# Pooled attention and two gated layers on one core: the second layer's block products changed from eight to seven

## The chip, the cores and the metric

One core of one Trainium2 chip. A core has a matrix engine (PE, with its weight loader PEld), a vector engine (DVE), an activation engine (ACT), a general engine (POOL), a queue that only issues transfers (SP), and 16 DMA engines. The metric is device time in microseconds (us) of one execution; lower is better. The kernel before takes 1918.09 us (median of three runs, 1917.99 to 1919.66).

## The reference

```python
def _attn_ref(q, k, v):                 # 8 batches, 8 heads, 576 positions, head size 64
    k_p, v_p = mean over groups of 8 positions of k, v
    attn = softmax(q @ k_p.T / sqrt(64))
    return attn @ v_p
def _moe_ref(x, w_in, w_out):           # 4608 tokens, 512 -> 2048 -> 512
    h = x @ w_in
    return (h * clip(h + 3, 0, 6) / 6) @ w_out
def _moe2_ref(x, w_gate, w_val, w_out): # 512 -> 1536 -> 512
    g = x @ w_gate
    return (g / (1 + exp(-g)) * (x @ w_val)) @ w_out
```

The output is `_moe2_ref(_moe_ref(_attn_ref(q, k, v)))`, 4608 x 512 in float32. The weights come as float64.

## The kernel before

Activations are kept transposed: features on the 128 partitions, tokens along the free dimension, in nine blocks of N = 512 tokens. A float32 operand of a large product is held as a pair hi + lo of float32r values, and a product is three matmuls: hi hi, hi lo, lo hi (`mm3`, its matmul is line 460). `split` makes a pair: ACT casts hi (line 118), and DVE or POOL subtracts it for lo (line 119). A weight arrives as 64-bit words in pieces of 128 x 256 and is brought to float32 by bits: ACT rescales it (line 97) and DVE does three integer operations for each piece (`join`, lines 102, 108 and 113). `Weights.convert(n)` moves n pieces through each of the three stages fetched, rescaled, joined.

The order of every engine's instructions is the program's order; nothing is reordered by a planner. A tile pool has a fixed number of buffers, and whoever writes a buffer anew waits for the last reader of its tile before.

First layer: blocks j = 0 to 8, in each the 16 feature tiles f, called slots here. A slot issues `up` (12 matmuls into a bank `h`), half of the attention steps due for the next block (`attn_slot`), `act1` (ACT Relu, line 482, then DVE, line 484), a `convert`, `down1` of the slot two before (12 matmuls into four banks `y`), the other half of the attention steps, `emit_fly` (the split of this slot's down weights, cast on ACT, lo on POOL), `split_g` (g's own split), and a `convert`. Block 0 converts the first layer's weights, block 8 and the second layer's first block convert the second layer's. Attention has two banks of its own (`ps_a`, tag `att`); line 352 is the score product, lines 438 to 441 are attention's last products, lines 449 and 453 split their result into x.

Second layer: for each block j and each f of 12, 12 matmuls `gate`, 12 `val`, the activation (lines 522 to 525), the split of g on ACT and DVE, and 12 matmuls of `down2` of the f before. All its up weights lie in SBUF as pairs, its down weights as float32, split anew for every use by `emit_fly`. That makes 9 x 12 x 36 = 3888 matmuls of 512 columns.

Of the kernel before, what the change touches and what calls it, by code (L numbers as in the profile page):

```python
# [8 lines left out]
F32 = mybir.dt.float32  # L9
# [14 lines left out]
def kernel(  # L24
# [37 lines left out]
    wu_p = ctx.enter_context(tc.tile_pool(name="wu", bufs=F1))  # L62
    wd_p = ctx.enter_context(tc.tile_pool(name="wd", bufs=F1))
    fly_p = ctx.enter_context(tc.tile_pool(name="fly", bufs=2))
    stg_p = ctx.enter_context(tc.tile_pool(name="stg", bufs=6))
    x_p = ctx.enter_context(tc.tile_pool(name="x", bufs=2))
    g_p = ctx.enter_context(tc.tile_pool(name="g", bufs=2))
    t_p = ctx.enter_context(tc.tile_pool(name="t", bufs=2))
    dram = ctx.enter_context(tc.tile_pool(name="dram", bufs=1, space=DRAM))
    ps_y = ctx.enter_context(tc.tile_pool(name="ps_y", bufs=1, space=PSUM))  # L70
    ps_h = ctx.enter_context(tc.tile_pool(name="ps_h", bufs=2, space=PSUM))
    ps_a = ctx.enter_context(tc.tile_pool(name="ps_a", bufs=2, space=PSUM))
# [4 lines left out]
    y_d = [dram.tile([P, KT, N], F32, name=f"y{j}") for j in range(NB)]  # L77

# [1 line left out]
    wu = {}  # L80
    wd = {}
# [11 lines left out]
    # Scaled by 2^-112, the high word's view as float32 has its exponent field  # L93
    # at float32's bias, three bits too low.
# [26 lines left out]
    class Weights:  # L121
        """Pieces of weight tiles, fetched ahead and converted in order."""
# [21 lines left out]
        def convert(self, n=1):  # L144
            """Moves each of three stages on by n pieces, the last stage first."""
            done, self.joined = self.joined, []
            for (kind, key, _, pool, i), t in done:
                if kind == "up":
                    if i == 0:
                        self.cur[key] = pool().tile([P, 2, KT, P], F32R, tag="wu", name="wu")  # L150
                    w = self.cur[key].rearrange("p a k f -> p a (k f)")[:, :, WC * i:WC * (i + 1)]
                    split(w[:, 0], w[:, 1], f32(t), nc.gpsimd)
                if i == KT * P // WC - 1:
                    (wu if kind == "up" else wd)[key] = self.cur.pop(key)
            pieces = []
            scaled, self.scaled = self.scaled, []
            for item, s in scaled:
                kind, key, _, pool, i = item
                if kind == "up":
                    t = t_p.tile([P, WC], I32, tag="w32", name="w32")  # L160
                else:
                    if i == 0:
                        self.cur[key] = wd_p.tile([P, DM], F32, tag="wd", name="wd")
                    t = self.cur[key][:, WC * i:WC * (i + 1)].bitcast(I32)
                pieces.append((s, t))
                self.joined.append((item, t))
# [10 lines left out]
    def emit_fly(key):  # L177
        t = fly_p.tile([P, 2, DM], F32R, tag="fly", name="fly")
        split(t[:, 0], t[:, 1], wd[key], nc.gpsimd)
        fly[key] = t  # L180

# [9 lines left out]
    a_p = attn_ctx.enter_context(tc.tile_pool(name="a", bufs=1))  # L191
# [35 lines left out]
    # The first batch is staged whole, in the up weights' place.  # L227
# [54 lines left out]
    # Before the first block the products' banks are free for the attention.  # L282
# [196 lines left out]
    # first layer  # L479
# [15 lines left out]
    def store_y(j):  # L495
        for d in range(KT):
# [5 lines left out]
            (nc.sync if d % 2 else nc.scalar).dma_start(out=y_d[j][:, d], in_=o)  # L502

    # second layer
    x2_t = {}

    y_t = {}

    def load_y(j):
        for kt in range(KT):  # L510
            y_t[j, kt] = p2["y"].tile([P, N], F32, tag="ystg", name="ystg")
            nc.sync.dma_start(out=y_t[j, kt], in_=y_d[j][:, kt])

    def split_y(j, kt):
        if kt == 0:
            x2_t[j] = x_p.tile([P, KT, 2, N], F32R, tag="x", name="x2")
        x = x2_t[j]
        split(x[:, kt, 0], x[:, kt, 1], y_t.pop((j, kt)), nc.vector)

    def act2(pg, pv):  # L520
        s = t_p.tile([P, N], F32, tag="t", name="s")
        nc.scalar.activation(out=s, in_=pg, func=ACTF.Sigmoid)  # L522
        u = t_p.tile([P, N], F32, tag="g32", name="u")
        nc.vector.tensor_tensor(out=u, in0=s, in1=pg, op=ALU.mult)  # L524
        nc.vector.tensor_tensor(out=u, in0=u, in1=pv, op=ALU.mult)  # L525
        return u

    def down2(j, f):
        if f == 0:
            accumulators((2, j))  # L530
        g, w = g_t.pop((2, j, f)), fly.pop(("out2", f))
        for i in range(N // P):
            mm3(acc[2, j][i], lambda _, a: g[:, a, i * P:(i + 1) * P], lambda _, a: w[:, a],
                [0], f == 0, f == F2 - 1)

    def store_o(j):
        for i in range(N // P):
            o = t_p.tile([P, DM], F32, tag="t" if i % 2 else "g32", name="oo")
            if i % 2:
                nc.vector.tensor_copy(out=o, in_=acc[2, j][i])  # L540
            else:
                nc.scalar.copy(out=o, in_=acc[2, j][i])
            nc.sync.dma_start(out=out[j * N + i * P:j * N + (i + 1) * P, :], in_=o)

# [1 line left out]
    # Attention units (batch, head pair, first query, queries, queries per  # L546
    # tile), none across a block's edge, in the order of the blocks.
# [62 lines left out]
    # The order must keep every stage behind what it reads, and every buffer  # L610
    # until its last reader.
# [112 lines left out]
    def wu_pool():  # L724
        return wu_p

    with tc.manual_schedule():
# [20 lines left out]
        for f in range(F1):  # L748
            weights.add_up(("in", f), w_in, wu_pool, f)
            weights.add_down(("out", f), w_out, f)  # L750
# [5 lines left out]
        while ("out", 0) not in wd:  # L756
            weights.convert(2)
# [9 lines left out]
        early = 8  # L767
        p2 = {}
        seq1 = [(j, f) for j in range(NB) for f in range(F1)]
        for n, (j, f) in enumerate(seq1):  # L770
            if j == NB - 1 and f == 0:
                attn_ctx.close()
                p2["pool"] = ctx.enter_context(tc.tile_pool(name="wu2", bufs=early))
                p2["y"] = ctx.enter_context(tc.tile_pool(name="ystg", bufs=4))
                for m in range(F2):
                    for i, (nm, src) in enumerate((("gate", w_gate), ("val", w_val))):
                        pool = p2["pool"] if 2 * m + i < early else wu_p
                        weights.add_up((nm, m), src, lambda pool=pool: pool, m)
                    weights.add_down(("out2", m), w_out2, m)
# [4 lines left out]
            weights.convert({0: 2, NB - 1: 2}.get(j, 0))  # L784
# [9 lines left out]
            if j == NB - 1 and f == 4:  # L794
                load_y(0)
            if j == NB - 1 and 8 <= f < 8 + KT:
                split_y(0, f - 8)
# [4 lines left out]
        weights.convert(2)  # L802
# [55 lines left out]
```

## Time and profile before

| | |
|---|---|
| median of three runs | 1918.09 us |
| span of the profiled execution, first to last instruction | 1917.7 us |
| PE, PEld busy | 1844.3 (96%), 1520.1 (79%) |
| DVE, ACT, POOL busy | 1052.7 (55%), 707.9 (37%), 630.4 (33%) |
| data moved | 95.96 MB, mean 50 GB/s |
| chain that ended last | PE 81%, DVE 12%, issue 3%, DMA 2%, ACT 1%, POOL 1% |

The page holds the busy shares, the span in 40 slices, and the chain of waits that ended last. Other views group instructions by line and shape, list who waited for whom, show instructions in order of time, or give each engine's busy time in chosen stretches with the clock that PE was granted (1.00 is 2.4 GHz, 0.50 is 1.2 GHz). A busy time counts an instruction from start to end, and waiting for a port lies inside it.

### The profile page before, as it was taken

The page shows a single profiled execution, that of the slowest core. Times are in us where ns is not written, and L with a number is a line of the kernel's source. Part 1 is how long each engine was busy: PE and PEld are TensorE (multiplying, and loading weights), DVE is VectorE, ACT ScalarE, POOL GpSimd, SP SyncE. Part 2 cuts the span into 40 slices and gives each one's busy share as a digit, 9 for nine tenths or more (in the row PEclk, how much of TensorE's full clock was granted, in tenths as well). Part 3 has the DMA queues.
Part 4 walks back from the last instruction along what each step waited for, and adds up shares of the span by engine and source line. Part 5 has one row for each costly group of instructions (what it writes and reads, how often), then busy time and mean ns, then how long its engine had stood idle before and what let it go on. Part 6 is the DMA issues. An engine that isn't in the chain of part 4 may idle for free.

```text
span 1917.7 us, 24136 instructions
## 1 busy us (share of the span) xinstructions
PE 1844.3 (96%) x8525; PEld 1520.1 (79%) x8525; DVE 1052.7 (55%) x1975; ACT 707.9 (37%) x1712; POOL 630.4 (33%) x730
## 2 busy tenths in 40 slices
PE   5787999999999999999988999999999999999999
PEld 4666788888888888788776788888888888888887
DVE  7999676666577766754698723232323332323322
ACT  5444444444444444444454422222222222222222
POOL 5556453535435353622343311111111111111111
PEclk8789999999999999999999999999999999999999
DMA  7443112111111121210245110101010101000000
GB/s 163 122 148 109 47 44 56 44 48 47 43 34 47 49 53 33 45 55 1 88 143 165 55 44 0 45 1 44 1 45 0 44 1 31 14 22 23 8 16 22
DMA packets 136553, 95.96 MB, mean 50 GB/s; under 512 B 84720, under 2 KB 105200, under 8 KB 136432
## 3 DMA queue, kind: packets, MB, share of 16 engines
q1 hardware_dynamic: 131728, 89.43, 16.4%
q10 hardware_dynamic: 4704, 4.98, 0.8%
q8 instruction: 67, 1.10, 0.2%
q14 instruction: 54, 0.44, 0.1%
HBM read 75.50 MB, written 18.87 MB: 49 GB/s over the span
## 4 chain that ended last, share of the span: by engine, by line
PE 81%; DVE 12%; issue 3%; DMA 2%; ACT 1%; POOL 1%; SPq 0%; POOLq 0%; DVEq 0%; ACTq 0%
PE y L460 31%; PE h L460 17%; PE val L460 14%; PE gate L460 14%; DVE w L108 2%; PE pss L352 2%; DVE wd L108 2%; DVE wd L102 2%; DVE w L102 1%; DVE w L113 1%; DVE wd L113 1%; PE pst L412 1%; PE pst L416 1%; DVE g L484 1%; POOL wu L119 1%
## 5 line engine op out<-in xcount | busy, mean ns | idle before, releaser
L119 POOL TENSOR_TENSOR fly<-wd,fly 128x512 fp32r<-128x512 f32 x252 | 331.8, 1317 | 809.1 <-ACT fly L118 804.9
L460 PE MATMUL h<-x,wu 128*128 128x512 f32 x1728 | 439.2, 404 | 9.5 <-DVE g L484 9.5
L460 PE MATMUL y<-g,fly 128*128 128x512 f32 x1728 | 429.1, 397 | 4.5 <-ACT g L118 2.4
L460 PEld LDWEIGHTS h<-x,wu 128*128 128x128 f32 x1728 | 324.7, 193 | 77.3 <-DVE g L484 12.0
L460 PEld LDWEIGHTS y<-g,fly 128*128 128x128 f32 x1728 | 317.5, 189 | 69.1 <-DVE g L119 3.2
L460 PE MATMUL y<-fly,g 128*128 128x512 f32 x1296 | 312.9, 390 | 3.4 <-POOL fly L119 3.4
L460 PE MATMUL gate<-x,wu 128*128 128x512 f32 x1296 | 311.3, 389 | 0.0
L460 PE MATMUL val<-x,wu 128*128 128x512 f32 x1296 | 311.3, 389 | 0.0
L460 PEld LDWEIGHTS y<-fly,g 128*128 128x128 f32 x1296 | 242.8, 188 | 56.1 <-POOL fly L119 5.7
L460 PEld LDWEIGHTS gate<-x,wu 128*128 128x128 f32 x1296 | 243.3, 188 | 50.5
L460 PEld LDWEIGHTS val<-x,wu 128*128 128x128 f32 x1296 | 243.3, 188 | 50.4
L524 DVE TENSOR_TENSOR u<-s,gate 128x512 f32<-128x512 f32 x108 | 74.1, 686 | 340.0 <-ACT s L522 340.0
L522 ACT ACTIVATE s<-gate 128x512 f32<-128x512 f32 x108 | 64.4, 596 | 331.0 <-PE gate L460 331.0
L118 ACT CAST g<-u 128x512 fp32r<-128x512 f32 x108 | 67.0, 621 | 309.2 <-DVE u L525 309.2
L119 DVE TENSOR_TENSOR g<-g,g 128x512 fp32r<-128x512 f32 x128 | 132.7, 1037 | 84.9 <-ACT g L118 84.9
L395 POOL TENSOR_TENSOR e<-e,sm 96x288 f32<-96x288 f32 (+3 forms) x85 | 68.1, 801 | 336.9 <-ACT g L118 151.6
L118 ACT CAST fly<-wd 128x512 fp32r<-128x512 f32 x252 | 155.1, 615 | 27.0 <-PE y L460 26.1
L525 DVE TENSOR_TENSOR u<-u,val 128x512 f32<-128x512 f32 x108 | 74.2, 687 | 135.9 <-PE val L460 135.0
L119 DVE TENSOR_TENSOR g<-u,g 128x512 fp32r<-128x512 f32 x108 | 74.8, 693 | 79.2 <-ACT g L118 79.2
L484 DVE SCALAR_TENSOR_TENSOR g<-t,h 128x512 f32<-128x512 f32 x144 | 97.2, 675 | 30.5 <-ACT t L482 28.7
L382 ACT ACTIVATE e<-e 96x288 f32<-96x288 f32 (+3 forms) x85 | 35.3, 415 | 190.7 <-DVE e L379 188.4
L482 ACT ACTIVATE t<-h,three 128x512 f32<-128x512 f32 x144 | 98.1, 681 | 19.4 <-PE h L460 19.0
(97 smaller groups left out, 1708.8 us busy)
## 6 DMA issues: line engine op xcount, KB each, us to landing
wstg<-in_moe_w_out_dram SPq DMA_DIRECT2D x56, 256.0 KB
ystg<-y SPq DMA_DIRECT2D x36, 256.0 KB
out_dram<-oo SPq DMA_DIRECT2D x36, 256.0 KB
wstg<-in_moe_w_in_dram SPq DMA_DIRECT2D x32, 256.0 KB
k_in<-in_k_dram SPq DMA_DIRECT2D x56, 144.0 KB
wstg<-in_moe_w_gate_dram SPq DMA_DIRECT2D x24, 256.0 KB
wstg<-in_moe_w_val_dram SPq DMA_DIRECT2D x24, 256.0 KB
y<-yo ACTq DMA_DIRECT2D x18, 256.0 KB
```

The source lines that it names most:

```text
L102: nc.vector.tensor_scalar(out=dst, in0=hi, scalar1=4, scalar2=1, op0=ALU.logical_shift_left, op1=ALU.logical_shift_right,)
L108: nc.vector.scalar_tensor_tensor(out=dst, in0=lo, scalar=29, in1=dst, op0=ALU.logical_shift_right, op1=ALU.bitwise_or)
L113: nc.vector.scalar_tensor_tensor(out=dst, in0=hi, scalar=-(2 ** 31), in1=dst, op0=ALU.bitwise_and, op1=ALU.bitwise_or)
L118: nc.scalar.copy(out=hi, in_=src)
L119: lo_engine.tensor_tensor(out=lo, in0=src, in1=f32(hi), op=ALU.subtract)
L395: nc.gpsimd.tensor_tensor(out=e3, in0=e3, in1=sm.to_broadcast(list(e3.shape)), op=ALU.mult)
L460: nc.tensor.matmul(out=ps, lhsT=w(kt, wh), rhs=x(kt, xh), start=first and n == 0, stop=last and n == 3 * len(kts) - 1,)
L482: nc.scalar.activation(out=t, in_=ps, func=ACTF.Relu, bias=three)
L484: nc.vector.scalar_tensor_tensor(out=g, in0=t, scalar=6.0, in1=ps, op0=ALU.min, op1=ALU.mult)
L522: nc.scalar.activation(out=s, in_=pg, func=ACTF.Sigmoid)
L524: nc.vector.tensor_tensor(out=u, in0=s, in1=pg, op=ALU.mult)
L525: nc.vector.tensor_tensor(out=u, in0=u, in1=pv, op=ALU.mult)
```

## The change

The second layer works on six groups of 768 tokens, and each of its three products on 2 x 2 blocks, with seven block products in place of eight (Strassen's scheme in Winograd's form). The sums of weight blocks are built, split into pairs and written to DRAM during the first layer's blocks 1 to 7, one of 18 units in six slots (`prep_step`); in the second layer all of them are streamed back for every group through a ring of four SBUF tiles (`load_up`, `load_dn`). The first layer's down weights are split once, in block 0, written to DRAM, and loaded again for each later slot (`load_fly`).

```diff
-    wd_p = ctx.enter_context(tc.tile_pool(name="wd", bufs=F1))
-    fly_p = ctx.enter_context(tc.tile_pool(name="fly", bufs=2))
+    fly_p = l1.enter_context(tc.tile_pool(name="fly", bufs=3))
...
+    M = 384
+    NG = NT // (2 * M)
+    NPAIR = F2 // 2
...
         def convert(self, n=1):
...
+                if i == 0:
+                    if kind == "up":
+                        self.cur[key] = wu_p.tile([P, 2, KT, P], F32R, tag="wu", name="wu")
+                    else:
+                        self.cur[key] = fly_p.tile([P, 2, DM], F32R, tag="fly", name="fly")
...
+                split(w[:, 0], w[:, 1], f32(t), nc.gpsimd)
                 if i == KT * P // WC - 1:
+                    t = self.cur.pop(key)
+                    (wu if kind == "up" else fly)[key] = t
+                    if kind == "down":
+                        nc.sync.dma_start(out=w1_d[key[1]], in_=f32(t))
...
-    def emit_fly(key):
+    def load_fly(f):
         t = fly_p.tile([P, 2, DM], F32R, tag="fly", name="fly")
-        split(t[:, 0], t[:, 1], wd[key], nc.gpsimd)
+        nc.sync.dma_start(out=f32(t), in_=w1_d[f])
...
+    def prep_step(u, step):
...
+        elif step == 2:
+            q = prep_t["f"] = q7_p.tile([P, 8, WC], F32, tag="q7", name="q7")
+            join([(s, q[:, i].bitcast(I32)) for s, i in prep_t.pop("q")])
...
+        elif step == 4:
+            nc.scalar.copy(out=t[:, :, 0], in_=q[:, :7])
+        else:
+            for a, b, eng in ((0, 4, nc.gpsimd), (4, 7, nc.vector)):
+                eng.tensor_tensor(out=t[:, a:b, 1], in0=q[:, a:b], in1=f32(t[:, a:b, 0]), op=ALU.subtract)
...
+    def x_step(p, n, lo_eng, sum_eng):
...
+        split(x[:, 0], x[:, 1], v(what), lo_eng)
+        if then:
+            sums_b(sum_eng, v, (then,))
...
+    def up2(p, u):
+        f, m = u
+        for what, wa, xb in UP:
+            b = bank()[:, :M]
+            w, x = wr.pop(("up", u, A7[wa])), xc[p, xb]
+            for k in range(2):
+                mm3x(b, lambda a: w[:, a, k], lambda a: x[:, a, k], k == 0, k == 1)
...
+    def split_gc(p, n, c, lo_eng):
+        what = DN[n][1]
+        t = gc[p, n, c] = l2["gc"].tile([P, 2, CH, M], F32R, tag="gc", name="gc")
+        split(t[:, 0], t[:, 1], gf[p][:, GP[what], CH * c:CH * (c + 1)], lo_eng)
+    def sums_g(p, what, eng):
+        h = NPAIR // 2
+        for a in range(0, NPAIR, h):
+            sums_a(eng, lambda q: gf[p][:, GP[q], a:a + h], (what,))
+    def down2(p, n):
+        what = DN[n][0]
+        b = dn_b[what] = [bank()[:, :2 * P] for i in range(PT)]
+        for c in range(NPAIR // CH):
+            g = gc.pop((p, n, c))
+            for t in range(PT):
+                for k in range(CH):
+                    w = wr["dn", n, CH * c + k]
+                    mm3x(b[t], lambda a: g[:, a, k, t * P:(t + 1) * P], lambda a: w[:, a],
+                         c == 0 and k == 0, c == NPAIR // CH - 1 and k == CH - 1)
...
             hp = ps_h.tile([P, N], F32, tag="h", name="h")
             up(hp, wu["in", f], x_tile(j))
             attn_slot(j, 2 * f)
             g = act1(hp)
-            weights.convert({0: 2, NB - 1: 2}.get(j, 0))
+            weights.convert(2 if j == 0 else 0)
             if n >= 2:
                 jd, fd = seq1[n - 2]
                 down1(jd, fd)
...
-            emit_fly(("out", f))
             split_g((1, j, f), g)
-            weights.convert({0: 2, NB - 1: 2 * (f % 2)}.get(j, 0))
+            weights.convert(2 if j == 0 else 0)
+            if j > 0 and n - F1 < PREP_STEPS * len(preps):
+                prep_step((n - F1) // PREP_STEPS, (n - F1) % PREP_STEPS)
+            if j == NB - 1 and f >= 4 and f < 11:
+                x_step(0, f - 4, nc.gpsimd, nc.gpsimd)
...
+        for p in range(NG):
+            for n, (f, m) in enumerate(units2):
+                c = up2(p, (f, m))
+                load_next()
+                if m == 0:
+                    g = gate2(c)
+                else:
+                    val2(p, f, g, c)
+                    if f % CH == CH - 1:
+                        split_gc(p, 0, f // CH, nc.gpsimd)
+                        split_gc(p, 1, f // CH, nc.vector)
+                if n == 2 and p + 1 < NG:
+                    load_y(p + 1, y_pool)
+            NC = NPAIR // CH
+            for n in range(7):
+                down2(p, n)
+                load_next()
+                evac(p, n)
+                if n == 0:
+                    for c in range(NC):
+                        split_gc(p, 2, c, nc.vector)
+                    sums_g(p, "S1", nc.vector)
+                    sums_g(p, "S3", nc.vector)
+                    sums_g(p, "S2", nc.vector)
+                elif n < 5:
+                    if n == 3:
+                        sums_g(p, "S4", nc.vector)
+                    for c in range(NC):
+                        split_gc(p, n + 2, c, nc.vector)
+                if p + 1 < NG:
+                    x_step(p + 1, n, nc.gpsimd, nc.gpsimd)
```

Of `prep_step`, step 0 issues four fetches of 256 KB, step 1 four rescales on ACT, and step 3 four sums of 128 x 256 on POOL. `units2` are 12 units, gate and val of six pairs f. In `up2` each of the seven products has a bank of its own: ACT copies P1, and DVE adds the others (P7 twice). `evac` makes three ACT copies for P1 and P4 and three DVE adds of 128 x 256 for each other product, six for P7. `gate2` has four Sigmoids on ACT, one product on DVE and three on POOL, all of 128 x 384; `val2` the same products without the Sigmoids. The eight PSUM banks are one ring in the second layer.

## Rows read from the trace of the kernel before

**Rows 1.** The page, busy time and share of the span.

```profile
PE 1844.3 (96%) x8525; PEld 1520.1 (79%) x8525; DVE 1052.7 (55%) x1975; ACT 707.9 (37%) x1712; POOL 630.4 (33%) x730
```

**Rows 2.** Windows: length, busy PE, PEld, DVE, ACT, POOL; clock, DMA share, GB/s.

```profile
52.90:204.20 151.30, 121.76 (x578) 97.09 (x578) 140.49 (x287) 70.31 (x198) 87.45 (x104) 0.87 0.38 114
204.20:916.50 712.30, 712.30 (x3541) 594.31 (x3541) 465.95 (x941) 319.80 (x823) 307.63 (x392) 1.00 0.17 43
916.50:1027.30 110.80, 96.78 (x410) 76.90 (x409) 92.98 (x172) 59.34 (x134) 46.04 (x45) 0.98 0.37 122
1027.30:1127.00 99.70, 96.76 (x422) 78.46 (x421) 65.98 (x125) 37.50 (x87) 33.85 (x32) 1.00 0.25 82
1127.00:1907.00 780.00, 780.00 (x3443) 646.09 (x3442) 245.49 (x330) 189.02 (x330) 123.22 (x96) 1.00 0.07 21
```

**Rows 3.** Waits, 60 to 204 and 916 to 1027: us in total, times, longest.

```profile
PE pss L352 <- DVE x L453: 16.5, 6, 5.4
...
PE h L460 <- DVE g L484: 9.5, 6, 2.3
```

**Rows 4.** Timeline: start, length; four matmuls of 256 columns, two of 128.

```profile
453.07 0.28 PE L438 MATMUL psv<-aT,vst 128*128 128x256 f32 x1
...
453.42 0.28 PE L441 MATMUL psv<-aTt,vtl 96*128 96x256 f32 x1
...
403.40 0.28 PE L440 MATMUL psv<-aT,vst 128*128 128x128 f32 x1
403.51 0.27 PE L441 MATMUL psv<-aTt,vtl 96*128 96x128 f32 x1
```

**Rows 5.** Lines by shape: busy us, mean ns, for DVE sources in PSUM.

```profile
L525 DVE TENSOR_TENSOR u<-u,val 128x512 f32<-128x512 f32 x108 | 74.2, 687 | 135.9 <-PE val L460 135.0
...
L453 DVE TENSOR_TENSOR x<-psv,x 128x256 fp32r<-128x256 f32 x32 | 13.4, 418 | 18.8 <-ACT x L449 18.8
```

**Rows 6.** Tile g: ns shortest, median, longest; DVE with both sources in SBUF.

```profile
L119 DVE TENSOR_TENSOR g<-g,g x128: 667/818/2728, 213.3 to 1022.6; 128x512 fp32r<-128x512 f32 x128
...
L119 DVE TENSOR_TENSOR g<-u,g x108: 691/693/694, 1035.2 to 1909.2; 128x512 fp32r<-128x512 f32 x108
```

**Rows 7.** Tile w: the conversion's operations, ns shortest, median, longest.

```profile
L102 DVE TENSOR_SCALAR w<-wstg x80: 249/286/1424, 34.2 to 1082.3; 128x256 int32<-128x256 int32 x80
L108 DVE SCALAR_TENSOR_TENSOR w<-wstg,w x80: 406/414/3392, 34.9 to 1083.9; 128x256 int32<-128x256 int32 x80
L113 DVE SCALAR_TENSOR_TENSOR w<-wstg,w x80: 406/412/1504, 35.7 to 1084.5; 128x256 int32<-128x256 int32 x80
L118 ACT CAST wu<-w x80: 388/406/423, 38.4 to 1085.0; 128x256 fp32r<-128x256 f32 x80
L119 POOL TENSOR_TENSOR wu<-w,wu x80: 717/749/2770, 38.9 to 1087.9; 128x256 fp32r<-128x256 f32 x80
```

**Rows 8.** Tile wd: cast and lo of the down weights' split.

```profile
L118 ACT CAST fly<-wd x252: 601/617/632, 61.8 to 1909.1; 128x512 fp32r<-128x512 f32 x126
L119 POOL TENSOR_TENSOR fly<-wd,fly x252: 1255/1290/1753, 62.5 to 1909.8; 128x512 fp32r<-128x512 f32 x126
```

**Rows 9.** Timeline of half a slot in block 0: start, length.

```profile
129.14 3.01 PE L460 MATMUL y<-g,fly 128*128 128x512 f32 x12
...
129.50 0.70 ACT L118 CAST wu<-w 128x256 fp32r<-128x256 f32 x2
...
130.42 1.25 DVE L102 TENSOR_SCALAR wd<-wstg 128x256 int32<-128x256 int32 x2
130.72 1.53 POOL L119 TENSOR_TENSOR wu<-w,wu 128x256 fp32r<-128x256 f32 x2
```

**Rows 10.** Windows, a stall of PE in block 0 and the clock behind it.

```profile
62.50:66.00 3.50, 0.00 (x0) 0.00 (x0) 3.50 (x6) 2.01 (x6) 2.77 (x2) 1.00 0.00 0
67.00:70.30 3.30, 3.30 (x10) 2.56 (x9) 3.30 (x10) 1.59 (x4) 1.48 (x2) 0.50 0.87 291
```

**Rows 11.** Windows, the second layer's first 8 us: DMA share, GB/s.

```profile
1027.00:1035.00 8.00, 8.00 (x37) 6.58 (x37) 6.07 (x15) 4.10 (x11) 4.29 (x4) 1.00 0.75 252
```

More of the change, by code (lines that the diff above doesn't have):

```diff
@@ L175, with sums_a @@
     fly = {}
-    def emit_fly(key):
+    def load_fly(f):
         t = fly_p.tile([P, 2, DM], F32R, tag="fly", name="fly")
-        split(t[:, 0], t[:, 1], wd[key], nc.gpsimd)
-        fly[key] = t
+        nc.sync.dma_start(out=f32(t), in_=w1_d[f])
+        fly["out", f] = t
+    A7 = {"11": 0, "S2": 1, "S1": 2, "12": 3, "22": 4, "S3": 5, "S4": 6, "21": 7}
+    B7 = {"11": 0, "T1": 1, "21": 2, "T2": 3, "22": 4, "T3": 5, "T4": 6, "12": 7}
+    def sums_a(eng, v, ops=("S1", "S3", "S2", "S4")):
+        for what in ops:
+            a, b, op = {
+                "S1": ("21", "22", ALU.add), "S3": ("11", "21", ALU.subtract),
+                "S2": ("S1", "11", ALU.subtract), "S4": ("12", "S2", ALU.subtract),
+            }[what]
+            eng.tensor_tensor(out=v(what), in0=v(a), in1=v(b), op=op)
@@ L520, in act2 @@
[L520 to L528, printed above, removed]
-        if f == 0:
[L530 to L543, printed above, removed]
+            (nc.sync if d % 2 else nc.scalar).dma_start(out=y_d[:, d, j * N:(j + 1) * N], in_=o)
+    UP = [("P1", "11", "11"), ("P6", "S2", "T2"), ("P5", "S1", "T1"), ("P2", "12", "21"),
+          ("P4", "22", "T4"), ("P7", "S3", "T3"), ("P3", "S4", "22")]
@@ new lines, with load_y @@
+    DN = [("P1", "11", "11"), ("P4", "22", "T4"), ("P2", "12", "21"), ("P6", "S2", "T2"),
+          ("P5", "S1", "T1"), ("P7", "S3", "T3"), ("P3", "S4", "22")]
+    HALF = 4
+    CH = 2
+    l2 = {}
+    xc, ys, gf, gc, wr = {}, {}, {}, {}, {}
+    def load_y(p, pool):
+        t = pool()
+        for quarter in ("11", "12", "21", "22"):
+            r, c = int(quarter[0]) - 1, int(quarter[1]) - 1
+            t0 = 2 * M * p + M * c
+            nc.sync.dma_start(out=t[:, 2 * r + c], in_=y_d[:, 2 * r:2 * r + 2, t0:t0 + M])
+        ys[p] = t
@@ new lines, in ring_tile, with load_up @@
+    def ring_tile():
+        return l2["ring"].tile([P, 2048], F32R, tag="wr", name="wr")
+    def load_up(u):
+        f, m = u
+        src = s_up[f][m].rearrange("p s a k f -> p s (a k f)")
+        for h, (a, b) in enumerate(((0, HALF), (HALF, 7))):
+            t = ring_tile()
+            nc.sync.dma_start(
+                out=f32(t[:, :512 * (b - a)]), in_=src[:, a:b].rearrange("p s n -> p (s n)")
+            )
+            for s in range(a, b):
+                wr["up", u, s] = t[:, 512 * (s - a):512 * (s - a + 1)].rearrange("p (a k f) -> p a k f", a=2, k=2)
@@ new lines, in load_dn, with bank @@
+    def load_dn(n):
+        s = B7[DN[n][2]]
+        src = s_dn[:, s].rearrange("p f a n -> p (f a n)")
+        for h in range(2):
+            t = ring_tile()
+            k = NPAIR // 2 * 512
+            nc.sync.dma_start(out=f32(t[:, :k]), in_=src[:, k * h:k * (h + 1)])
+            for f in range(NPAIR // 2):
+                wr["dn", n, NPAIR // 2 * h + f] = t[:, 512 * f:512 * (f + 1)].rearrange("p (a n) -> p a n", a=2)
+    def bank():
+        return l2["ps"].tile([P, 512], F32, tag="b", name="b")
@@ new lines, in mm3x, with tmp @@
+    def mm3x(ps, w, x, first, last):
+        for n, (wh, xh) in enumerate(((0, 0), (0, 1), (1, 0))):
+            nc.tensor.matmul(out=ps, lhsT=w(wh), rhs=x(xh), start=first and n == 0, stop=last and n == 2)
+    def tmp(tag):
+        return l2["t"].tile([P, M], F32, tag=tag, name=tag)
+    def up2(p, u):
+        f, m = u
+        add = lambda dst, a, b: nc.vector.tensor_tensor(out=dst, in0=a, in1=b, op=ALU.add)
+        for what, wa, xb in UP:
[3 more added lines that the diff above has]
+                mm3x(b, lambda a: w[:, a, k], lambda a: x[:, a, k], k == 0, k == 1)
+            if what == "P1":
+                c11 = tmp(f"c11{m}")
+                nc.scalar.copy(out=c11, in_=b)
+            elif what == "P6":
+                c21 = tmp(f"c21{m}")
+                add(c21, c11, b)
+            elif what == "P5":
+                c12 = tmp(f"c12{m}")
+                add(c12, c21, b)
+            elif what == "P2":
+                add(c11, c11, b)
+            elif what == "P4":
+                add(c21, c21, b)
+            elif what == "P7":
+                c22 = tmp(f"c22{m}")
+                add(c22, c12, b)
+                add(c21, c21, b)
+            else:
+                add(c12, c12, b)
+        return {"11": c11, "22": c22, "21": c21, "12": c12}
@@ new lines, with gate2 @@
+    TURN = {"11": "11", "22": "22", "21": "12", "12": "21"}
+    GP = {"11": 0, "S2": 0, "12": 1, "S4": 1, "21": 2, "S3": 2, "22": 3, "S1": 3}
+    def gate2(c):
+        g = {}
+        for q in ("11", "22", "21", "12"):
+            g[q] = tmp("s" + q)
+            nc.scalar.activation(out=g[q], in_=c[q], func=ACTF.Sigmoid)
+        for q in ("11", "22", "21", "12"):
+            eng = nc.vector if q == "11" else nc.gpsimd
+            eng.tensor_tensor(out=g[q], in0=g[q], in1=c[q], op=ALU.mult)
+        return g
@@ new lines, with evac, out_tile, add @@
+    o_t = {}
+    def evac(p, n):
+        what = DN[n][0]
+        b = dn_b[what]
+        def out_tile(tag):
+            o_t[tag] = l2["o"].tile([P, PT, 2 * P], F32, tag=tag, name=tag)
+            return o_t[tag]
+        def add(dst, a):
+            for t in range(PT):
+                nc.vector.tensor_tensor(out=dst[:, t], in0=a[:, t], in1=b[t], op=ALU.add)
+        def copy(dst):
+            for t in range(PT):
+                nc.scalar.copy(out=dst[:, t], in_=b[t])
+        def store(tag, r, c):
+            t0 = 2 * M * p + M * r
+            nc.sync.dma_start(
+                out=out[t0:t0 + M, 2 * P * c:2 * P * (c + 1)].rearrange("(t p) d -> p t d", p=P),
+                in_=o_t[tag],
+            )
+        if what == "P1":
+            copy(out_tile("o12"))
+        elif what == "P4":
+            copy(out_tile("o21"))
+        elif what == "P2":
+            add(out_tile("o11"), o_t["o12"])
+            store("o11", 0, 0)
+        elif what == "P6":
+            add(o_t["o12"], o_t["o12"])
+            nc.gpsimd.tensor_tensor(out=o_t["o21"], in0=o_t["o21"], in1=o_t["o12"], op=ALU.add)
+        elif what == "P5":
+            add(o_t["o12"], o_t["o12"])
+        elif what == "P7":
+            add(o_t["o21"], o_t["o21"])
+            add(out_tile("o22"), o_t["o12"])
+            store("o21", 1, 0)
+            store("o22", 1, 1)
+        else:
+            add(o_t["o12"], o_t["o12"])
+            store("o12", 0, 1)
@@ L746 @@
             nc.gpsimd.memset(t, 0.0)
-        for f in range(F1):
-            weights.add_up(("in", f), w_in, wu_pool, f)
-            weights.add_down(("out", f), w_out, f)
+        for f in range(F1 + 1):
+            if f < F1:
+                weights.add_up(("in", f), w_in, f)
+            if f:
+                weights.add_down(("out", f - 1), w_out, f - 1)
         load_first(segs[0][3])
@@ L755 @@
         startup[0] = False
-        while ("out", 0) not in wd:
+        while ("in", 1) not in wu:
             weights.convert(2)
@@ L765, in attn_slot, with x_pool, load_next @@
                 run_steps(block_end[j] + upto)
-        early = 8
-        p2 = {}
+        def x_pool():
+            return x_p.tile([P, 4, 2, M], F32, tag="x", name="ystg")
+        units2 = [(f, m) for f in range(NPAIR) for m in range(2)]
+        stream = [("up", u) for u in units2] + [("dn", n) for n in range(7)]
+        sent = [0]
+        def load_next():
+            if sent[0] < NG * len(stream):
+                kind, what = stream[sent[0] % len(stream)]
+                (load_up if kind == "up" else load_dn)(what)
+                sent[0] += 1
         seq1 = [(j, f) for j in range(NB) for f in range(F1)]
@@ L772 @@
                 attn_ctx.close()
[L773 to L779, printed above, removed]
+                prep_ctx.close()
+                l2["x"] = ctx.enter_context(
+                    tc.tile_pool(name="xc", bufs=1, side="right", reuse_waits="tile"))
+                l2["ring"] = ctx.enter_context(
+                    tc.tile_pool(name="wr", bufs=4, side="right", reuse_waits="tile"))
+                load_y(0, x_pool)
+            if j > 0:
+                load_fly(f)
             hp = ps_h.tile([P, N], F32, tag="h", name="h")
```

157 lines of the change are left out of this document (86 added, 71 removed).

## The prediction

> **What bounds the kernel now.** The page comes first [rows 1]: PE is busy for 96% of the span, DVE for 55%. An average hides the stages, so the windows are cut where blocks begin [rows 2]. There are four states. Block 0 takes 151.3 us, with DVE busy for 140.5 of them and PE for 121.8. Blocks 1 to 7 have PE without a gap, 712.3 of 712.3, and DVE at 65%. Block 8 has PE at 96.8 of 110.8 and DVE at 93.0. The second layer is PE alone: 780.0 of 780.0 at clock 1.00, 3443 matmuls, so 226.5 ns each. The list of waits tells what PE waits for in the two stages with gaps [rows 3]: in block 0 for an attention bank that DVE frees at line 453, in block 8 for DVE's line 484, both behind the integer operations of the weight conversion. So the second layer pays for matmul columns, block 0 for DVE and block 8 for conversion.
>
> **Matmuls.** Removed: 3888 matmuls, 880.6 us at 226.5 ns. Added: 12 units x 7 products x 6 x 6 groups = 3024 of 384 columns, and 7 products x 54 x 6 groups = 2268 of 256. Before has 256 columns in attention: three steps take 0.35 us, 117 ns each [rows 4]. Two of 128 columns stand 110 ns apart in the same rows, so a change of weights alone has a floor of about 110 ns and 256 columns lie just above it. For 384 the middle of 117 and 226.5 is 172 ns. Sum: 3024 x 172 = 520 us, 2268 x 117 = 265 us, 785 us together. Bounds: by columns from the 512 row (170 and 113 ns) 770; at 120 ns, one reading of the 256 row, 792. The second layer ran from 1027.3 us to 1913.9, 886.6 us with its own small gaps.
>
> The Trainium skill (TensorE: Matmul & The Clock Gate, section Back-to-back issue gap) gives N/2.4 + 2.5 ns warm, which makes 739 us of this sum and 839 of the layer before. The row shows 226.5 ns where it gives 216, so the row decides here.
>
> **DVE and POOL beside them.** Where both sources of a DVE operation lie in SBUF, its length depends on POOL. The lo of g takes 691 to 694 ns in the second layer; in the first, beside a busy POOL, the median is 818 and the longest 2728 [rows 6]. In the timeline a pair of conversions (free 286 each) takes 1.25 us because POOL holds two operations beside it [rows 9]. Sources in PSUM show no such spread: 687 for 512 columns, 418 for 256 [rows 5]. I therefore add DVE's SBUF work to POOL's instead of laying the one beside the other. By lines through rows 5 to 8: DVE 0.55 us for 384 columns, 0.97 for 768, 1.40 for 1152; ACT cast 0.83 for 768; POOL 1.02 for 384, 1.83 for 768.
>
> A pair of up units is 84 x 172 ns = 14.5 us of PE. DVE has 14 additions from PSUM and two products, of 0.55 each, and half a lo: 9.3 us. POOL has six products and half a lo, 7.0 us, which meet 1.6 us of DVE's SBUF work. Both fit, and eight banks cover a delay of seven products. Nothing is added there.
>
> A down phase is 7 x 54 x 117 ns = 44.2 us of PE, 6.3 a product. DVE has 16 lo (15.5), eight sums (11.2) and 18 PSUM additions (7.5); POOL in `x_step` and `evac` has 12 operations of 1.83 (22.0). Together 56.2 us do not fit into 44.2. Followed in order, with T the end of the up phase: the last chunk of P1's operand waits for three POOL products and a lo, some 1 us late. ACT copies P1 at T+7.7 and only then casts P2's operand; DVE has its three lo at T+11.4. Then six sums, 8.4, with two POOL operations between, 3.7: T+23.5. The sixth operand's first lo is there at T+24.4, and PE wanted it at T+19.9: 4.5 us of stall. For P7 the same chain (lo of P5, three additions of P6, the two sums S4, and four POOL operations) ends at T+41 to 42 where PE stands at T+37: 5 us. A stall of 3.5 us in block 0 was followed by 3.3 us at clock 0.50 [rows 10], but PE catches up to DVE anyway, so 1 us for it. That is 11.5 us for each of five groups and 1.5 for the last, which has no `x_step`: 59. Ends: 10 if POOL's work falls into DVE's gaps, 95 if both stalls are doubled. One us for the banks that the first layer's results still hold. Second layer: 785 + 59 + 1 = 845, 41.6 less than 886.6.
>
> **The stream.** 33 MB a group is 198 MB, with y and the output 217 MB in 845 us, 257 GB/s. Before moved 252 GB/s at a DMA share of 0.75 [rows 11]; in proportion the limit is 336. A unit's half is asked for one unit and more ahead (5 us to spare). Cost 0; if 250 were the limit, the layer would take 868.
>
> **Block 8.** Its 408 matmuls need 92.4 us at 226.5 ns and it takes 110.8 [rows 2]. The conversion leaves, POOL gets `x_step` instead, and DVE has only the activation. Gain 18.4; at the worst 10. PE is late next, by its own work.
>
> **Block 0.** DVE's joins stay. Two waits are added. The split of f + 1's down weights needs the third-last `fly` buffer, which `down1` of f - 2 reads, and that is issued behind it: in the slot shown `y` ends at 132.15 and ACT's casts began at 129.50 [rows 9], 2.7 us. ACT's rescales, attention copies and the cast of g are queued behind that wait, and DVE's next join behind POOL's lo. Second, every join now writes the two small tiles that the pair of lo just issued reads. For 13 slots this is at most 3.5 us each, 45; nothing where PE has run ahead of DVE, as after its waits. POOL's lo costs 1.5 us for 1.3 before [rows 7, 8]. I take 20, the nearer end to the stage that is already waiting on the port.
>
> **Blocks 1 to 7.** Gone are a cast of 0.62 and a POOL lo of 1.29 a slot [rows 8]; PE has no gap there, so they are worth nothing. Added, once in six slots: a join of 12 operations, 4 x (0.29 + 0.41 + 0.41) = 4.4 us free [rows 7], say 5.5 with POOL beside it, 8 at the worst; also four rescales, one cast of 1792 columns, four POOL sums and two lo, in slots of their own. DVE is free for 35% of these 6.4 us slots. Attention banks are reused two half slots later, about 6 us, or one half slot where a k product stands between. So 18 bursts cost between 0 and 2.5 us: I take 8 in all, 45 the upper end. Loads of `fly` (512 KB) have two slots to land; behind SP's waits for them stand the k, q and v loads, with a unit to spare.
>
> **Sum.** 1917.7 - 41.6 - 18.4 + 20 + 8 = 1885.7 in the profiled execution, whose span is 0.4 below the median of the runs: 1886 us.
>
> **Rivals.** (a) Layer one pays: the 12-operation joins push DVE's line 453 behind, PE stalls 3 us on a bank at each, and each stall halves the clock as in rows 10 (another 2): 18 x 5 = 90 in place of 8. For it: this is the wait of rows 3. Against it: there a join comes every half slot, here every sixth slot. Time 1968, slower than before; it decides from (1917.7 - 1877.7) / 18 = 2.2 us a burst. (b) The port costs little: 10 in place of 59, and block 0 only 5: 1886 - 49 - 15 = 1822. For it: POOL's own lengths hardly grow [rows 8]. Against: 2728 in rows 6. (c) The stream is the limit at 250 GB/s: the layer takes 868, 1909 in all; rows 11 speak against it. (d) Matmuls under 512 columns lose what they have over columns at 2.4 GHz (12 ns of 172, and 7 of 117 down to the 110 of the weights): 3024 x 12 + 2268 x 7 = 52 us less, 1834. The 117 itself is against it [rows 4]. By the skill's rule above it would be 46 less.
>
> **How the numbers follow.** Forecast with its neighbours 0.54, (a) or block 0 at its upper end together with doubled stalls 0.24, (b) 0.13, (c) 0.07, (d) 0.02. The forecast's own range, from the ends of the down phase, block 0 and the joins, is 1845 to 1925. To leave out no more than 2 in 10 the range goes from 1835 to 1950. A difference under 0.2% (3.8 us) could not be told from none. Faster: the forecast but for 0.03 of its upper end, (b), (d) and most of (c), 0.70; same 0.05; slower 0.25.
>
> **What would show it.** Matmuls of 256 columns 117 ns and of 384 columns 172 ns apart in the second layer; PE gaps at the fourth and sixth product of each down phase that end on DVE's or ACT's split, and none in the up units; lo and sums of DVE lengthened where POOL works; block 8 near 93 us; block 0 near 170; blocks 1 to 7 near 720. It is wrong if PE waits for the ring's DMA, if PE has gaps in blocks 1 to 7 that sum to over 40 us, or if the down phases take under 47 us or over 65.

## The result: slower, and the profile after

The changed kernel is 0.8% slower. It takes 1933.36 us (median of four runs, 1931.0 to 1935.99) against 1918.04 us (four runs, 1916.5 to 1919.66): a ratio of 1.0082, 95% interval 1.0066 to 1.0098. Forecast was 1886. The profiled execution has a span of 1929.3 us. Its page, against [rows 1]:

```profile
PE 1783.5 (92%) x9929; PEld 1601.3 (83%) x9929; DVE 1306.6 (68%) x2455; ACT 687.7 (36%) x1612; POOL 850.5 (44%) x858
```

PE has less work and more gaps. The windows of the same stages say where, against [rows 2]; a row is start and end, length, busy time of PE, PEld, DVE, ACT and POOL, then clock, DMA share and GB/s. The first three are blocks 0, 1 to 7 and 8; then come one up phase, one down phase, and the whole second layer:

```profile
56.10:212.80 156.70, 123.18 (x579) 99.23 (x579) 121.17 (x287) 71.61 (x214) 86.54 (x119) 0.88 0.50 160
212.80:983.60 770.80, 734.29 (x3541) 603.60 (x3540) 511.90 (x1175) 314.65 (x801) 278.34 (x370) 0.98 0.58 182
983.60:1076.10 92.50, 92.50 (x409) 76.60 (x408) 24.78 (x36) 30.46 (x46) 20.23 (x11) 1.00 0.44 157
1076.10:1163.50 87.40, 87.40 (x506) 87.38 (x505) 56.12 (x97) 20.56 (x41) 41.23 (x36) 1.00 0.76 265
1163.50:1219.20 55.70, 47.20 (x380) 46.39 (x380) 48.27 (x44) 20.55 (x30) 36.01 (x16) 0.94 0.60 208
1076.10:1925.40 849.30, 805.51 (x5293) 801.02 (x5291) 609.63 (x841) 240.87 (x414) 435.97 (x295) 0.98 0.73 251
```

| stage | before | forecast | after |
|---|---|---|---|
| start | 52.9 | 52.9 | 56.1 |
| block 0 | 151.3 | 171 | 156.7 |
| blocks 1 to 7 | 712.3 | 720 | 770.8 |
| block 8 | 110.8 | 92.4 | 92.5 |
| second layer | 886.6 | 845 | 849.3 |
| tail | 3.8 | 3.8 | 3.9 |

The second layer and block 8 bring 55.6 us, where 60 were forecast. Blocks 1 to 7 take 58.5 back, where 8 were forecast; start and block 0 take 8.6. The 58.5 us have two parts, by the busy times of PE in the windows: PE has gaps of 770.8 - 734.3 = 36.5 us, and the same 3541 matmuls are busy for 734.3 us instead of 712.3 [rows 2], 22.0 us longer, at a mean clock of 0.98 instead of 1.00.

**What PE and its neighbours wait for in blocks 1 to 7.** The four largest of PE's own waits (us in total, times, longest; the line numbers are those of the changed kernel):

```profile
PE psv L524 <- DVE aT L518: 6.9, 6, 2.7
PE psk L382 <- DVE e L465: 5.3, 5, 2.2
PE y L546 <- DMA fly<-w1d: 5.2, 2, 2.8
PE y L546 <- ACT x L535: 4.1, 1, 4.1
```

In the whole list most waits end with a step of attention on DVE or ACT; 5.2 us end with a reload of down weights. Now the waits of ACT, and those of SP (SPq is SP issuing a transfer) in the same stretch:

```profile
ACT wstg L115 <- DMA wstg<-in_moe_w_gate_dram: 19.7, 16, 5.1
ACT wstg L115 <- DMA wstg<-in_moe_w_val_dram: 17.3, 21, 4.7
ACT wstg L115 <- DMA wstg<-in_moe_w_out_dram: 9.6, 9, 3.6
```

```profile
SPq L354 <- DVE qT L425: 94.8, 25, 8.4
SPq L199 <- PE y L546: 71.2, 22, 6.1
SPq L310 <- ACT vtl L416: 60.9, 19, 8.1
...
SPq L266 <- DVE s L259: 37.7, 6, 8.8
SPq L261 <- DVE s L259: 34.8, 12, 7.3
```

ACT waits 46.6 us at line 115, the rescale, for staged weights that have not landed. SP waits for buffers of q (line 354), of the reloaded down weights (199) and of v's tail (310), and for the sums to be finished before it stores them (261, 266). The timeline around one unit's rescale shows how SP's lateness becomes ACT's (start, length, engine; in brackets the idle time before):

```profile
314.44 2.00 SPq L104 DMA_DIRECT2D wstg<-in_moe_w_gate_dram  x4
...
316.54 0.89 SPq L199 DMA_DIRECT2D fly<-w1d  x2
...
317.42 0.44 ACT L115 ACTIVATE wstg<-wstg 128x256 f32<-128x256 f32 x1 [5.08 <-DMA wstg<-in_moe_w_gate_dram]
...
318.79 0.43 ACT L115 ACTIVATE wstg<-wstg 128x256 f32<-128x256 f32 x1 [0.94 <-DMA wstg<-in_moe_w_gate_dram]
320.50 0.43 ACT L115 ACTIVATE wstg<-wstg 128x256 f32<-128x256 f32 x1 [1.28 <-DMA wstg<-in_moe_w_gate_dram]
...
321.21 0.43 ACT L115 ACTIVATE wstg<-wstg 128x256 f32<-128x256 f32 x1 [0.29 <-DMA wstg<-in_moe_w_gate_dram]
321.55 0.43 ACT L468 ACTIVATE e<-e 96x288 f32<-96x288 f32 x1
...
322.01 0.45 DVE L475 TENSOR_REDUCE sm<-e 96x4 f32<-96x288 f32 x1 [6.34 <-ACT e L468]
...
323.05 1.17 PE L546 MATMUL y<-g,fly 128*128 128x512 f32 x4 [2.83 <-DMA fly<-w1d]
```

The slot whose end holds this unit's step 0 began at 297.5 us on PE; the four fetches leave SP at 314.4, 16.9 us later, where a slot takes about 6.6. From 312.3 to 321.6 ACT does nothing but wait and rescale. The exp of attention (line 468) and the Relu of g stand behind it on ACT, DVE waits 6.3 us for the exp, and PE has a gap of 2.8 us. That row names the reload as what ended this gap; the reload stood directly behind the fetches in SP's queue (line 199, 316.54).

**The second layer.** PE's row for an up phase, 504 matmuls in 87.4 us, is 173.4 ns each; a down product without a stall takes 6.3 us for 54, 116.7 ns (the down phase of experiment 8, 379 in 44.28 us, gives 116.8). In the down phase the list of PE's waits and rows of four tiles read as follows (ns shortest, median, longest; `gf` holds the gated activations and their sums, `gc` their split, `ystg` the first layer's result and its sums, `xc` their split). The last row is the same POOL operation in block 8, where DVE is busy for 24.8 of 92.5 us:

```profile
PE b L653 <- DVE gc L137: 5.6, 2, 4.8
PE b L653 <- ACT gc L136: 1.8, 1, 1.8
PE b L653 <- POOL gc L137: 1.1, 1, 1.1
```

```profile
L137 DVE TENSOR_TENSOR gc<-gf,gc x16: 946/1324/2608, 1166.4 to 1214.7; 128x768 fp32r<-128x768 f32 x16
L215 DVE TENSOR_TENSOR gf<-gf x8: 1347/1678/3007, 1175.1 to 1199.3; 128x1152 f32<-128x1152 f32 x8
...
L137 POOL TENSOR_TENSOR xc<-ystg,xc x7: 2040/2563/2928, 1174.7 to 1211.4; 128x768 fp32r<-128x768 f32 x7
L220 POOL TENSOR_TENSOR ystg<-ystg x4: 2427/2568/2838, 1177.0 to 1204.0; 128x768 f32<-128x768 f32 x4
...
L137 POOL TENSOR_TENSOR xc<-ystg,xc x7: 1840/1847/1847, 1012.5 to 1045.1; 128x768 fp32r<-128x768 f32 x7
```

A sum takes 1347 ns when POOL is idle and up to 3007 beside it, and POOL's operations are longer too, 2.0 to 2.9 us where 1.83 was reckoned and 1.84 to 1.85 measured in block 8: each is longer while the other works.

### The profile page after: what moved, and what is told of

It is laid out like the page before. It is cut to its first block, busy times and chain, and to the rows that moved or that the text cites. A ratio compares the mean times of both kernels' runs of the same rounds, so it can differ in the third digit from the quotient of the medians.

```text
span 1929.3 us, 28452 instructions
## 1 busy us (share of the span) xinstructions
PE 1783.5 (92%) x9929; PEld 1601.3 (83%) x9929; DVE 1306.6 (68%) x2455; ACT 687.7 (36%) x1612; POOL 850.5 (44%) x858
## 5 line engine op out<-in xcount | busy, mean ns | idle before, releaser
L653 PE MATMUL b<-xc,wr 128*128 128x384 f32 x3024 | 525.2, 334 | 0.0
L653 PEld LDWEIGHTS b<-xc,wr 128*128 128x128 f32 x3024 | 524.0, 188 | 0.1
L662 DVE TENSOR_TENSOR c<-c,b 128x384 f32<-128x384 f32 x504 | 270.6, 553 | 168.8 <-PE b L653 165.9
L653 PE MATMUL b<-wr,gc 128*128 128x256 f32 x2268 | 282.1, 286 | 43.7 <-DVE gc L137 27.9
L653 PEld LDWEIGHTS b<-wr,gc 128*128 128x128 f32 x2268 | 277.6, 195 | 48.0 <-DVE gc L137 30.0
L701 POOL TENSOR_TENSOR s<-s,c 128x384 f32<-128x384 f32 x108 | 118.0, 1119 | 208.6 <-ACT s L698 208.6
L137 DVE TENSOR_TENSOR gc<-gf,gc 128x768 fp32r<-128x768 f32 x108 | 155.8, 1482 | 59.9 <-ACT gc L136 59.7
L709 POOL TENSOR_TENSOR gf<-s,c 128x384 f32<-128x384 f32 x108 | 118.1, 1122 | 124.3 <-DVE c L662 124.3
L136 ACT CAST gc<-gf 128x768 fp32r<-128x768 f32 x126 | 99.2, 833 | 205.2 <-DVE gf L709 123.4
L137 POOL TENSOR_TENSOR xc<-ystg,xc 128x768 fp32r<-128x768 f32 x42 | 99.3, 2374 | 138.0 <-ACT xc L136 138.0
L698 ACT ACTIVATE s<-c 128x384 f32<-128x384 f32 x144 | 74.0, 525 | 156.7 <-DVE c L662 154.9
```

What stands on the lines that cost most here:

```text
L136: nc.scalar.copy(out=hi, in_=src)
L137: lo_engine.tensor_tensor(out=lo, in0=src, in1=f32(hi), op=ALU.subtract)
L653: nc.tensor.matmul(out=ps, lhsT=w(wh), rhs=x(xh), start=first and n == 0, stop=last and n == 2)
L662: add = lambda dst, a, b: nc.vector.tensor_tensor(out=dst, in0=a, in1=b, op=ALU.add)
L698: nc.scalar.activation(out=g[q], in_=c[q], func=ACTF.Sigmoid)
L701: eng.tensor_tensor(out=g[q], in0=g[q], in1=c[q], op=ALU.mult)
```

## Experiments

Two theories stand against each other for blocks 1 to 7. A: the fetches leave SP late, ACT waits for them in order, and all behind it is late. B, the mechanism of rival (a): the join's 12 DVE operations hold the attention's banks. The second layer has a theory of its own, that DVE's and POOL's work adds up.

Experiments 1 to 7 are single executions, so a repeat is needed to read small differences. Traces with the same first-layer program give one: blocks 1 to 7 take 770.8 us with the change and 767.3 in experiment 7, 732.6 in experiment 5 and 734.6 in experiment 8. Up to the start of block 1 the program is the same in the changed kernel and in all eight experiments; in these nine traces block 1 starts between 211.7 and 216.8 us. Differences of 3 to 4 us in a stage of the first layer are therefore not told apart from a repeat.

**1. Fetch earlier** (tests A against B).

```diff
         if step == 0:
-            place = A7 if kind == "up" else B7
...
+            if u == 0:
+                prep_fetch(0)
...
                 sums_b(nc.gpsimd, lambda n: q[:, B7[n]])
+            if u + 1 < len(preps):
+                prep_fetch(u + 1)
```

> The four fetches of a unit are issued three slots earlier (at step 3 of the unit before); nothing else changes. Theory A (the fetches leave SP's queue late, ACT waits for them at the rescale, 46.6 us in blocks 1 to 7, and everything behind it on ACT and then PE is late): blocks 1 to 7 fall from 770.8 us to 715 to 735, ACT's wait on the staged weights to under 5. Theory B (the join of 12 DVE operations holds attention's banks): they stay at 760 or more. The rest of the span unchanged within 5.

Measured: 1897.5 us; blocks 1 to 7 and the second layer:

```profile
214.20:950.00 735.80, 720.57 (x3541) 596.20 (x3540) 513.25 (x1175) 311.25 (x801) 278.23 (x370) 1.00 0.62 191
1042.50:1891.90 849.40, 814.59 (x5293) 807.58 (x5291) 610.04 (x840) 241.38 (x414) 435.82 (x295) 0.98 0.74 251
```

The list of waits has no row left for line 115. The same instructions, with the same traffic, take 35.0 us less, and the clock of the stretch is back at 1.00. A holds for 35 of the 58.5 us (31.5 against the repeat of 767.3), though the time is 0.8 above the range expected for it. 23.5 us are left: 15.2 of gaps and 8.3 of longer matmuls, by the busy time of PE.

**2. Join in two halves, fetch as late as before** (B alone).

```diff
-            join([(s, q[:, i].bitcast(I32)) for s, i in prep_t.pop("q")])
+            join([(s, q[:, i].bitcast(I32)) for s, i in prep_t["q"][:2]])
         elif step == 3:
             q = prep_t["f"]
+            join([(s, q[:, i].bitcast(I32)) for s, i in prep_t.pop("q")[2:]])
```

> The join of a unit is two halves of 6 DVE operations in two slots instead of one of 12; the fetches are as late as before. Theory A: blocks 1 to 7 stay at 760 to 775. Theory B: 735 or less, since a burst of 1.8 us fits into DVE's idle time.

Measured: 1927.9 us, blocks 1 to 7 767.3. That is 3.5 us less than with the change, and the same as the repeat without halves (767.3); ACT still waits 48.5 us at the rescale. B falls: the halves bring nothing that can be told from a repeat.

**3. No reload of the first layer's down weights** (what makes SP late?).

```diff
-            if j > 0:
-                load_fly(f)
+            if n == F1:
+                load_fly(f)
+                resident = fly["out", f]
+            elif j > 0:
+                fly["out", f] = resident
```

> Leaves out the reloads of the first layer's down weights: from block 1 on one loaded tile serves for all feature tiles (the sums are those of one weight tile). If SP is late because it waits in load_fly for PE (71 us of its waits) and because of 64 MB of traffic, the fetches arrive in time: blocks 1 to 7 at 715 to 740. If SP is late by its waits for q, k and v, as it was before the change, 755 or more.

This kernel leaves out the reloads and uses one tile's weights in all slots. Measured: 1910.6 us, blocks 1 to 7 750.0, in between the two expectations. ACT's wait at line 115 falls from 46.6 to 35.7. The reloads carry a part, 17 to 21 us, and most of ACT's wait is not due to them.

**4. The stores of finished sums from POOL's queue.**

```diff
-                nc.sync.dma_start(
+                nc.gpsimd.dma_start(
                     out=s_up[f][m].rearrange("p s a k f -> p (s a k f)"),
...
-                nc.sync.dma_start(out=s_dn[:, :, f], in_=f32(t))
+                nc.gpsimd.dma_start(out=s_dn[:, :, f], in_=f32(t))
```

> The fetches stay where the change has them; only the 18 stores of the finished sums are issued from POOL's queue in place of SP's. In SP's queue such a store stands directly ahead of the next unit's fetches and waits for DVE's and POOL's lo (89 us of SP's waits). If that wait makes the fetches late: ACT's 46.6 us of waits at the rescale fall under 20 and blocks 1 to 7 to 735 to 750. If SP is late by its waits for the attention's loads and the reloads: ACT's waits stay over 35 and the blocks over 760.

Measured: 1920.0 us, blocks 1 to 7 757.2, ACT's wait 38.8. The time is again in between, 10 to 14 us less by this store; ACT's wait stays over 35, as expected if SP is late by its other waits. Neither the reloads nor the store alone makes the fetch late; that the waits for q's, v's and k's buffers do the rest is argued from SP's list, and no run leaves them out.

**5 and 6. What the early fetch leaves.** Experiments 1 and 2 together, and 1 and 3 together (their edits as above).

> Early fetch and the join in halves together. Of the change's 58 us in blocks 1 to 7 the early fetch took 35 away, 23.5 were left (735.8 us against 712.3 before). If the join's burst is what is left, blocks 1 to 7 fall to 718 to 726; if the rest is traffic and SP's waits for the reloaded weights, they stay at 732 to 738.

> Early fetch, and the reloads of the down weights left out (one tile's weights serve for all). If the 23.5 us left in blocks 1 to 7 come from the reloads (64 MB of traffic, SP's waits for PE, 5 us of late reloads): 714 to 722 us. If they come from the conversion's own work on DVE, ACT and POOL: 730 or more.

Measured: 732.6 us in blocks 1 to 7 with the halves (1893.2 in all) and 728.5 without the reloads (1894.0). The first lies in the range expected if the join's burst is not what is left: it is worth 3.2 us at most, no more than a repeat differs. The second falls between its two ranges: the reloads are worth 7.3 us. Some 13 to 16 us stay open. PE's list in experiment 1 spreads its gaps over nine rows, of which this is the largest:

```profile
PE psv L534 <- DVE vtl L424: 4.9, 4, 2.9
```

That the rest lies in the conversion's other work (rescales, casts, POOL's sums) or in what it adds to the queues is argued, not shown.

**7. `x_step` on DVE** (the second layer).

```diff
-            nc.gpsimd.tensor_tensor(out=o_t["o21"], in0=o_t["o21"], in1=o_t["o12"], op=ALU.add)
+            nc.vector.tensor_tensor(out=o_t["o21"], in0=o_t["o21"], in1=o_t["o12"], op=ALU.add)
...
-                    x_step(p + 1, n, nc.gpsimd, nc.gpsimd)
+                    x_step(p + 1, n, nc.vector, nc.vector)
```

> x_step of the next group and the one o21 sum run on DVE instead of POOL (0.97 us for 1.85 each, and no port to share). Theory of the shared port (work of DVE and POOL adds up to 56 us in a down phase): it falls to 44 us, all on DVE, so a down phase with an x_step takes 46 to 49 us instead of 55.7, the second layer 805 to 820 instead of 849. Rival (DVE's own queue is the limit, the port only stretches what was hidden): 55 or longer. Blocks 0 to 8 unchanged.

Measured: 1893.2 us. The second layer, one down phase, and the two tiles in it:

```profile
1073.40:1887.20 813.80, 793.54 (x5293) 790.15 (x5291) 578.26 (x901) 241.41 (x414) 281.25 (x234) 1.00 0.77 262
1160.80:1209.60 48.80, 44.92 (x379) 44.32 (x378) 41.15 (x55) 20.68 (x30) 5.57 (x4) 1.00 0.74 245
```

```profile
L137 DVE TENSOR_TENSOR gc<-gf,gc x16: 949/952/1043, 1163.7 to 1203.2; 128x768 fp32r<-128x768 f32 x16
L215 DVE TENSOR_TENSOR gf<-gf x8: 1351/1351/1353, 1172.4 to 1194.8; 128x1152 f32<-128x1152 f32 x8
```

DVE got 12 operations more in each of five down phases (901 for 841 in the layer), and its busy time in the one shown fell from 48.27 to 41.15 us: the sums are 1351 to 1353 ns, none longer. The layer is 35.5 us shorter, and both times lie in the ranges expected. So DVE's and POOL's work on SBUF sources adds up here, as forecast, and the rival, DVE's own queue, falls.

**8. All of it, and the down phase in another order.** Experiments 1, 2 and 7, and

```diff
                 if n == 0:
-                    for c in range(NC):
-                        split_gc(p, 2, c, nc.vector)
                     sums_g(p, "S1", nc.vector)
                     sums_g(p, "S3", nc.vector)
+                    for c in range(NC):
+                        split_gc(p, 2, c, nc.vector)
                     sums_g(p, "S2", nc.vector)
                 elif n < 5:
-                    if n == 3:
-                        sums_g(p, "S4", nc.vector)
                     for c in range(NC):
                         split_gc(p, n + 2, c, nc.vector)
+                    if n == 1:
+                        sums_g(p, "S4", nc.vector)
...
-                        split_gc(p, 0, f // CH, nc.gpsimd)
+                        split_gc(p, 0, f // CH, nc.vector if f == NPAIR - 1 else nc.gpsimd)
```

> Early fetch, join in halves, x_step and o21 on DVE, and in the down phase three moves: S1 and S3 ahead of the split for P2 (DVE idles there 4 us for ACT), S4 two products earlier, the last lo of P1's operand on DVE. By the port theory a down phase needs 41 us of DVE beside 44.2 of PE and no operand is late any more: 44 to 46 us each, the second layer 790 to 800. Blocks 1 to 7 as with early fetch and halves, 718 to 736. Time 1840 to 1870, faster than both. If the waits only move to another product: down phase 48 or more and time 1875 or more.

Measured: 1836.77 us (four runs, 1835.9 to 1837.04), a ratio of 0.957 to the kernel before, interval 0.9553 to 0.9587. It beats both kernels; the time is 3 us under its range, the stages lie in theirs. Blocks 1 to 7, the second layer, and one down phase:

```profile
211.70:946.30 734.60, 722.69 (x3542) 598.26 (x3541) 507.95 (x1175) 311.50 (x801) 268.52 (x370) 0.99 0.62 191
...
1038.80:1830.20 791.40, 790.80 (x5293) 789.61 (x5291) 588.34 (x907) 243.22 (x414) 265.96 (x228) 1.00 0.79 269
1126.20:1170.60 44.40, 44.28 (x379) 44.08 (x378) 42.65 (x56) 20.98 (x30) 3.07 (x3) 1.00 0.79 266
```

PE is busy for 790.8 of 791.4 us in the second layer, with DVE at 42.65 of 44.4 in the down phase: the seven products now cost what their matmuls cost. The 22 us in blocks 1 to 7 are still there.

## Why the prediction was wrong, by its own steps

**The step that failed is "Blocks 1 to 7".** It priced the join, the rescales and the sums as bursts of 0 to 2.5 us with DVE's idle time as cover, and the fetches not at all. That the rescale stands one slot behind its fetch, that the fetch is issued in SP's order behind waits for DVE, ACT and PE, and that ACT takes nothing else meanwhile was not followed, though it named "SP's waits" for the reloads and gave the k, q and v loads behind them "a unit to spare". Those waits are in the kernel before too, here from SP's list for blocks 1 to 7:

```profile
SPq L268 <- DVE qT L339: 213.9, 32, 16.5
```

They cost nothing there: PE has no gap in that stretch. The fetches were the first thing in that queue with one slot of slack. The stage cost 58.5 us where 8 was taken and 45 the end: 35 by the late fetch (31.5 against the repeat; shown by experiment 1), 7 by the reloads (experiment 6), at most 3 by the join (not told from a repeat), the rest open. The prediction's own sign for this stage, gaps of PE over 40 us, was not met: the gaps are 36.5 us, and the other 22.0 lie in longer matmuls.

**Rival (a)** had the place and nearly the size (90 against 58.5; it decides from 2.2 us a unit, and 58.5 / 18 = 3.25), but the wrong mechanism: splitting the join brought no more than a repeat differs. That its size came near is luck in part. Its second half, that the gaps of PE come with a lower clock, was right: the mean clock of the stretch is 0.98 with the change and 1.00 with the early fetch. A unit lost 2.0 us in gaps and 1.2 in longer matmuls, for the 3 and 2 of this rival.

**Matmuls** were right: 173.4 and 116.7 ns where 172 and 117 were taken [rows 4]. 3024 x 173.4 + 2268 x 116.7 = 789 us for 785. Rival (d), without what they have over columns at 2.4 GHz, would have had 160 and 110; it fell. The Trainium skill (TensorE: Matmul & The Clock Gate, section Back-to-back issue gap) gives N/2.4 + 2.5 ns at full clock for an isolated matmul, an estimate of 162.5 and 109.2 ns here. The rows lie 7% above it, and the rows decide.

**DVE and POOL beside them** was right in mechanism and in sum, the sum in part by luck: a down phase takes 55.7 us where 44.2 + 11.5 was forecast, and the layer 849.3 where 845 was. But PE's waits are 8.5 us where 10.5 were forecast, and its matmuls are busy for 47.2 us where 44.2 was taken, 3 more, where 1 was taken for the clock; the two errors nearly cancel. The single waits were misplaced too. By the list of waits above, the last chunk for P1 was late by 1.1 us (POOL's part), the operand of P6 by 1.8 (ACT's cast) and by 0.8 once more within the product (DVE's part; its two waits sum to 5.6), where 4.5 was forecast at P6. The operand of P7 was late by 4.8, as forecast, and the clock then cost more than the 1 us taken. Two windows, the gap ahead of P7 and the matmuls behind it:

```profile
1200.00:1204.80 4.80, 0.02 (x1) 0.00 (x0) 4.80 (x3) 2.74 (x5) 4.72 (x3) 0.73 0.62 221
1204.90:1209.00 4.10, 4.10 (x19) 4.10 (x20) 4.10 (x2) 1.34 (x2) 4.10 (x3) 0.50 0.00 0
```

19 matmuls in 4.1 us are 216 ns each instead of 117. The product with this stall took 13.3 us for 6.3. The last group, which has no `x_step`, lost 1.4 us in its down phase, for 1.5 forecast. Rival (b), in which POOL's work falls into DVE's gaps, fell; its other half, 5 us for block 0, was met.

**The stream** was right: the up phases have no gap at 265 GB/s and a share of 0.76, so rival (c) fell; experiment 8 moves 269 GB/s at 0.79.

**Block 8** was right to 0.1 us. **Block 0** was overestimated: 5.4 us for 20, and 3.2 in the start; together 8.6, and 7.5 to 12.6 in the nine traces with this program. The wait for the third-last buffer is there, and small, three waits where up to 13 slots were reckoned:

```profile
ACT fly L136 <- PE y L546: 7.7, 3, 3.6
```

One thing there was not forecast at all: the same number of DVE operations, 287, is busy for 121.2 us instead of 140.5 [rows 2]. No run shows why.

In sum, with 1929.3 - 1885.7 = 43.6 us to explain: +50.5 in blocks 1 to 7, -11 in start and block 0, +4 in the second layer.

## What to carry to other kernels

A transfer added to a queue that issues in order is as late as the oldest buffer wait ahead of it: read that queue's own waits, and give each new load more slack than those ahead of it add up to, above all if an engine with other work consumes it in order. Here the longest single wait of the rows shown was 8.8 us, and a fetch left 16.9 us after its slot began. Before work is put on POOL to relieve DVE, add up what both do with two SBUF sources; if the sum exceeds the stage, the faster engine alone is better (48.8 us for 55.7 here). A saving in matmuls comes in full only when every operand is ready by the end of the product before it, so the order of the side work counts beside its amount (44.4 us a down phase for 48.8).

## What the runs showed of the hardware that was not expected

POOL's operations lengthen beside DVE too. In the kernel before only single ones did: the medians, 749 and 1290 ns, lie near the shortest, 717 and 1255, and the longest are 2770 and 1753 [rows 7, 8]. With both queues full of SBUF work, POOL's 768-column operations took 2040 to 2928 ns and DVE's 1152-column ones up to 3007, alternately: three of 768 columns on each took 7.6 us, 2.5 a pair, where the two take 0.95 and 1.84 alone:

```profile
1202.19 7.58 DVE L137 TENSOR_TENSOR gc<-gf,gc 128x768 fp32r<-128x768 f32 x3
...
1206.40 7.59 POOL L137 TENSOR_TENSOR xc<-ystg,xc 128x768 fp32r<-128x768 f32 x3
```

Giving DVE twelve more operations, and POOL twelve fewer, therefore shortened DVE's busy time by 7 us (experiment 7).
